# The beginning of an FFT filter and mixture-of-experts kernel laid out anew: larger loads of x, tables in order of use, one table made by transposes, weights later

## The chip, the cores and the metric

The kernel runs on one core of a Trainium2 chip. The metric is the device time of one execution in microseconds (us), the median of the runs shown; less is better.

## The reference

The input x has 8 sequences of 2496 rows and 256 channels. Each channel is filtered along its sequence in the frequency domain, and each filtered row then goes through one of 8 experts (a two-layer network), chosen by a gate.

```python
X = np.fft.rfft(x, axis=1)                    # x: 8 x 2496 x 256
y = np.fft.irfft(X * (filt_r + 1j * filt_i), n=2496, axis=1)
x = y.reshape(8 * 2496, 256)
logits = x @ w_gate                           # 256 x 8
probs = softmax(logits); e = argmax(logits)   # gate weight = probs[e]
out = probs[e] * (np.maximum(x @ w1[e], 0.0) @ w2[e])   # w1: 256 x 1024, w2: 1024 x 256
```

## The kernel before, in words

**The filter.** 2496 = 39 x 64, so the transform is done in two stages with matmuls. The work is cut into 16 units (u = 0 to 15): a sequence and one half of its channels. A unit has 5 iterations; t = 5u + it counts them from 0 to 79, and t is also the scale on which the whole program is ordered. For a unit, `loadx` (L231) brings x into tiles of 117 partitions (three groups of 39 rows) by 128 channels, and `forward1` (L249, matmul L257) multiplies by the small table `a1`; ScalarE, and for one of the six banks VectorE, copies the result out of PSUM into T (L265). A bank is up to 4 groups of x. For an iteration `spec1` transposes T (`pt`, L296) and ScalarE copies it to z (L302); `spec2` multiplies z by the second-stage table `bm` (`px`, L311); `filt_` multiplies by the filter `ff` on VectorE (`tr` and two halves of `ti`, L330 to L332); `join` adds the two on GpSimd (`p`, L339); `spec3` multiplies by the table `cm` (`pi`, L350), and ScalarE copies the result into the output tile U (L355). There are four tiles U0 to U3, a unit u using U(u mod 4).

**The tables.** `bm` and `cm` are 128 x 20 x 128 in f32, 0.26 MB for the four rows of an iteration, 1.31 MB each in all. `ff` holds the two parts of the filter: a DMA fills partitions 0 to 31 and 32 to 63 of it (L278 to L282), and `twice` (L287, instructions L289) copies them to partitions 64 to 127 on ScalarE, the second part with its sign turned, four rows (one iteration) at a time. Both units of a sequence and all sequences use the same tables. By construction cm for a row is the transpose of bm for it, except row 0.

**x in the beginning.** x goes through a pool of 4 buffers (`xp`) of one bank each, three DMAs of 78 KB to a bank. The load of a fifth bank waits until the first has been multiplied.

**The weights.** The experts' 16 weight matrices (0 to 15, w1 and w2 of each expert) are prepared while the filter runs: load (L373), VectorE maximum (L383), a turn through TensorE (`pw`, L406, and `pv`, L416) to get the maximum over partitions, split into a high half on ScalarE (L449) and a low half on VectorE (L454), and a write to a table `wscr` in HBM (L466, L468). In the order matrix q stands at t = 2.0 + 4.3 q.

**Behind it.** Once both units of a sequence are done its rows are routed, transformed to the time domain (`pg` L617, `py` L631) and scattered to `xs` in HBM by GpSimd (L158). From about t = 80 on the expert blocks are computed (`ph` L1014, `po` L1040) with weights loaded from `wscr` (L961).

**What sets the order.** All engines' queues are written out ahead of time, in the order of one list of steps, each with a key on the scale of t; `at(key, step)` puts a step there, and each engine goes through its part strictly in turn. So a step that must wait holds up all later steps of that engine, DMA issues on SyncE (SP) among them. What precedes t = 0 (the first loads, seven matmuls on a zero tile named `warm` at L750, the first unit's `forward1`) stands ahead of the list.

Of the kernel before, what the change touches and what calls it, by code (L numbers as in the profile page):

```python
# [9 lines left out]
F32 = mybir.dt.float32  # L10
# [5 lines left out]
ALU = mybir.AluOpType  # L16
# [11 lines left out]
GP = 3 * N1  # L28
# [85 lines left out]
def tile_fft_moe(ctx, tc, x, filt_r, filt_i, w_gate, w1, w2, cst, out):  # L114
    nc = tc.nc
# [24 lines left out]
    ident = cp.tile([128, 128], F32, name="ident")  # L140
# [44 lines left out]
    with ExitStack() as fctx:  # L185
# [42 lines left out]
        Uf = [u.rearrange("p n r -> p (n r)") for u in U]  # L228

        xt = {}  # L230

        def loadx(u, c):
            b, h = divmod(u, 2)
            xv = x[b].rearrange("(n1 n2) d -> n1 n2 d", n2=N2)[
                :, :, h * 128 : (h + 1) * 128
            ]
            t = xp.tile([GP, 4, 128], F32, name=f"x{u}_{c}", tag="x")
            g0, g1 = BANKS[c]
            for l in range(3):
                n = min(g1, NG if l == 0 else NG - 1) - g0  # L240
                s0 = 3 * g0 + l
                nc.sync.dma_start(
                    t[l * N1 : (l + 1) * N1, :n, :],
                    xv[:, s0 : s0 + 3 * (n - 1) + 1 : 3, :],
                )
# [24 lines left out]
        stk = {}  # L270
        ff = kp.tile([128, 2, 20, D], F32, name="ff")

        def loadf(k0, k1):

            n0 = max(k0, 1)
            for i, f in enumerate((filt_r, filt_i)):
                v = f[0:1248, :].rearrange("(j k) d -> j k d", k=N1)
                nc.sync.dma_start(ff[0:32, i, k0:k1], v[:, k0:k1, :])  # L278
                if k0 == 0:
                    nc.sync.dma_start(ff[32:33, i, 0], f[1248:1249, :])  # L280
                    nc.sync.dma_start(ff[33:64, i, 0], f[0:31, :])
                nc.sync.dma_start(  # L282
                    ff[32:64, i, n0:k1], v[:, 39 - n0 : 39 - k1 : -1, :]
                )

        def twice(k0, k1):

            for i, c in enumerate((1.0, -1.0)):
                nc.scalar.mul(ff[64:128, i, k0:k1], ff[0:64, i, k0:k1], c)  # L289
# [441 lines left out]
        def loadk(t, n, i0, i1, eng=nc.sync):  # L731
            eng.dma_start(t[:, 4 * i0 : 4 * i1], cst[n][:, 4 * i0 : 4 * i1])
# [24 lines left out]

        def consts():
# [21 lines left out]
        NU_ALL = 2 * B  # L780
# [3 lines left out]
        def at(key, f, *a):  # L784
            work.append((key, f, a))
# [14 lines left out]
                )  # L800


        K = {"s2": 1.394, "sr": 1.65, "si": 1.85, "s3": 3.6, "f": 0.063, "fd": 0.75, "w": 2.0, "wp": 4.3}
        RT = (0.0, 0.4, 0.45, 0.9, 1.3, 1.7, 2.2, 2.5, 2.9, 3.3)
        slow = lambda t: min(1.0, max(0.6, 1.0 - 0.06 * (t - 72)))
        for t in range(NT):
            u, it = divmod(t, 5)
            rho = slow(t)
            at(t, spec1, t)
            at(t + K["s2"] * rho, spec2, t)  # L810
            at(t + K["sr"] * rho, filt_, t)
            at(t + K["si"] * rho, join, t)
            at(t + K["s3"] * rho, spec3, t)
            if u + 1 < NU_ALL and it == 0:
                for j in range(6):
                    at(t + K["f"] + K["fd"] * j, forward1, u + 1, j)
            if u + 1 < NU_ALL and it == 0:
                for j in range(6):

                    n = 6 * (u + 1) + j - 4  # L820
                    v, i = divmod(n, 6)
                    at(5 * (v - 1) + K["f"] + K["fd"] * i + 0.02 if v else 0.01 + 0.02 * i, loadx, u + 1, j)
        for i in range(1, 5):
            if i > 1:
                at(0.1, loadk, bm, "bm", i, i + 1)
            if i % 2:
                at(0.09, loadf, 4 * i, 4 * i + 8)
            at(i - 0.1, twice, 4 * i, 4 * i + 4)
            at(0.1, loadk, cm, "cm", i, i + 1)

        PLACE = (80.0, 89.2, 109.2)
        done = []
        for b in range(B):
            rho = slow(10 * b + 9)
            s0 = 10 * b + 9 + K["s3"] * rho + 0.05
            c = 1.0 if b < B - 1 else 0.6
# [261 lines left out]
        for b in range(NB):  # L1098
            z, d, s = tau[b]
# [68 lines left out]
```

## Time and profile before

| what | value |
|---|---|
| median of 3 runs | 1451.44 us (1448.37, 1451.44, 1458.49) |
| the profiled execution | 1451.84 us, of which the span is 1450.1 us |
| TensorE (PE) matmul busy | 1334.0 us, 92% of the span |
| VectorE (DVE) busy | 823.5 us, 57% |
| ScalarE (ACT) busy | 855.7 us, 59% |
| GpSimd (POOL) busy | 456.3 us, 31% |
| PE busy in the first 60 us | 39.26 us |

The profile counts its times from the start of the span; the 1.74 us between the span and the execution's time lie around it. In rows of the timeline the first number is the start, the second the length, and what stands in brackets is the engine's idle time just ahead and what ended it. A matmul of f32 shows as two records, so that the four matmuls of a bank or of an iteration read as x8; a transpose shows as one, x4. PEclk is the granted TensorE clock, 1.00 at full speed. SPq is SyncE's queue, on which most DMAs are issued.

### The profile page before, as it was taken

The page shows a single profiled execution, that of the slowest core. Times are in us where ns is not written, and L with a number is a line of the kernel's source. Part 1 is how long each engine was busy: PE and PEld are TensorE (multiplying, and loading weights), DVE is VectorE, ACT ScalarE, POOL GpSimd, SP SyncE. Part 2 cuts the span into 40 slices and gives each one's busy share as a digit, 9 for nine tenths or more (in the row PEclk, how much of TensorE's full clock was granted, in tenths as well). Part 3 has the DMA queues.
Part 4 walks back from the last instruction along what each step waited for, and adds up shares of the span by engine and source line. Part 5 has one row for each costly group of instructions (what it writes and reads, how often), then busy time and mean ns, then how long its engine had stood idle before and what let it go on. Part 6 is the DMA issues. An engine that isn't in the chain of part 4 may idle for free.

```text
span 1450.1 us, 39859 instructions
## 1 busy us (share of the span) xinstructions
PE 1334.0 (92%) x14831; PEld 1189.0 (82%) x14831; DVE 823.5 (57%) x2381; ACT 855.7 (59%) x1449; POOL 456.3 (31%) x445
## 2 busy tenths in 40 slices
PE   5789999999989797789999998999999999999997
PEld 4777777777767576579999987998998998998997
DVE  0677878777676465245555554554554554554552
ACT  4557667666656554345666655565665655666564
POOL 1126484554737623521111111111111111111111
PEclk7799999999999899989999999999999999999999
DMA  7665565454533522367364289436436337234531
GB/s 193 177 189 175 165 180 171 156 172 152 170 120 113 178 67 68 94 185 201 75 160 111 74 231 329 108 77 161 102 78 188 72 79 187 74 78 125 137 78 42
DMA packets 199215, 199.07 MB, mean 137 GB/s; under 512 B 104259, under 2 KB 177652, under 8 KB 190700
## 3 DMA queue, kind: packets, MB, share of 16 engines
q1 hardware_dynamic: 179500, 153.80, 38.6%
q0 software_dynamic: 19520, 42.71, 10.5%
q8 instruction: 118, 1.93, 0.6%
q14 instruction: 77, 0.63, 0.2%
HBM read 347.54 MB, written 61.56 MB: 282 GB/s over the span
## 4 chain that ended last, share of the span: by engine, by line
PE 59%; DMA 6%; issue 4%; DVE 4%; ACT 2%; SPq 1%; POOL 1%; POOLq 0%; DVEq 0%; ACTq 0%
PE ph L1014 26%; PE po L1040 25%; DMA wb<-wscr 2%; PE py L631 2%; DMA wa<-wscr 2%; PE pi L350 1%; PE px L311 1%; PE pg L617 1%; PE f L257 1%; DMA xs<-yt,dest 1%; DVE hl L1028 1%; PE pt L296 1%; SPq L919 1%; DMA xt<-xs 0%; PE plw L481 0%
## 5 line engine op out<-in xcount | busy, mean ns | idle before, releaser
L1014 PE MATMUL ph<-xt,wa 128*128 128x128 f16 x7728 | 464.0, 219 | 28.1 <-DMA wa<-wscr 14.6
L1014 PEld LDWEIGHTS <-wa 128*128 128x128 f16 x7728 | 446.5, 98 | 41.3 <-issue 19.6
L1040 PE MATMUL po<-wb,hh 128*128 128x256 f16 x2576 | 435.3, 274 | 6.9 <-issue 2.6
L1028 DVE TENSOR_TENSOR hl<-hs,hh 128x512 f16<-128x512 f32 x322 | 223.7, 695 | 380.5 <-ACT hh L1022 316.6
L158 POOL DMA_INDIRECT out_dram<-ot,t x161 | 158.2, 983 | 696.7 <-DVE xs L994 621.6
L1040 PE MATMUL po<-wb,hl 128*128 128x256 f16 x1288 | 352.7, 274 | 3.1 <-issue 3.1
L1040 PEld LDWEIGHTS <-hh 128*128 128x128 f16 x2576 | 246.1, 98 | 40.4 <-issue 11.2
L1020 ACT ACTIVATE hs<-ph 128x512 f32<-128x512 f32 x322 | 191.8, 596 | 128.3 <-PE ph L1014 87.4
L158 POOL DMA_INDIRECT xs<-yt,dest x176 | 179.4, 1019 | 127.4 <-issue 56.7
L993 ACT ACTIVATE xs<-xb,s 128x256 f16<-128x256 f32 x161 | 81.8, 508 | 228.6 <-DVE s L983 224.0
L1022 ACT CAST hh<-hs 128x512 f16<-128x512 f32 x322 | 198.9, 618 | 10.1
L339 POOL TENSOR_TENSOR p<-tr,ti 128x512 f32<-128x512 f32 x80 | 107.1, 1338 | 160.2 <-DVE ti L332 120.2
L1040 PEld LDWEIGHTS <-hl 128*128 128x128 f16 x1288 | 126.5, 98 | 20.0 <-issue 4.9
L257 PE MATMUL f<-a,x 117*128 117x117 f32 x704 | 107.4, 297 | 26.0 <-DMA x<-in_x_dram 19.6
L257 PEld LDWEIGHTS f<-a,x 117*128 117x128 f32 x704 | 96.3, 209 | 32.7 <-issue 18.0
L355 ACT COPY U<-pi 128x512 f32<-128x512 f32 (+1 forms) x80 | 87.0, 1088 | 59.2 <-PE pi L350 44.8
L994 DVE SCALAR_TENSOR_TENSOR xs<-xb,s,xs 128x256 f16<-128x256 f32 x161 | 78.6, 488 | 53.5 <-ACT xs L993 53.1
L631 PE MATMUL py<-gh,dm 117*117 117x512 f32 x176 | 95.1, 622 | 8.9 <-ACT yt L633 6.5
L265 ACT COPY T<-f 128x468 f32<-128x468 f32 (+1 forms) x80 | 70.5, 881 | 51.6 <-PE f L257 50.7
L311 PEld LDWEIGHTS px<-z,bm 128*128 128x128 f32 x640 | 83.9, 201 | 15.4 <-issue 12.3
L350 PE MATMUL pi<-cm,p 128*128 128x128 f32 (+1 forms) x640 | 90.2, 286 | 4.8 <-POOL p L339 3.5
L311 PE MATMUL px<-z,bm 128*128 128x128 f32 x640 | 91.0, 288 | 0.2
(163 smaller groups left out, 1279.7 us busy)
## 6 DMA issues: line engine op xcount, KB each, us to landing
wb<-wscr SPq DMA_DIRECT2D x134, 1040.0 KB
wa<-wscr SPq DMA_DIRECT2D x134, 1024.0 KB
xb<-xs SPq DMA_DIRECT2D x161, 130.0 KB
x<-in_x_dram SPq DMA_DIRECT2D x240, 78.0 KB
wf<-in_moe_w_dram SPq DMA_DIRECT2D x32, 512.0 KB
wscr<-wh SPq DMA_DIRECT2D x8, 1040.0 KB
wscr<-wh SPq DMA_DIRECT2D x8, 1024.0 KB
xs<-yt,dest POOLq DMA_INDIRECT x176
```

Of the source, the lines that this page charges most:

```text
L158: nc.gpsimd.indirect_dma_start(out=dst, out_offset=bass.IndirectOffsetOnAxis(ap=idx, axis=0), in_=src, in_offset=None, bounds_check=bound, ...
L257: nc.tensor.matmul(ps[:, n : n + m], lhsT=xt.pop((u, g))[:m], rhs=a1[:m, :m], start=True, stop=True,)
L311: nc.tensor.matmul(ps[:, kk], lhsT=bm[:, 4 * it + kk], rhs=z[:, kk], start=True, stop=True,)
L339: nc.gpsimd.tensor_tensor(p, tr, ti, op=ALU.add)
L350: nc.tensor.matmul(ps[:, o : o + n], lhsT=p[:, kk], rhs=cm[:, k, :n], start=True, stop=True)
L355: nc.scalar.copy(U[u % NU].rearrange("p n r -> p r n")[:, r0 : r0 + o // 64, :], ps[:, :o].rearrange("p (r n) -> p r n", n=N2),)
L631: nc.tensor.matmul(ps[:GP], lhsT=dm, rhs=gh[:GP], start=True, stop=True)
L1014: nc.tensor.matmul(ps[:, f], lhsT=w[:, p : p + 128], rhs=xt[:, r, c], start=(n == 0), stop=(n == 5))
L1020: nc.scalar.activation(s, ps, AF.Relu, scale=1.0 / B23)
L1022: nc.scalar.copy(hh, s)
L1028: nc.vector.tensor_tensor(hl, s, hh, op=ALU.subtract)
L1040: nc.tensor.matmul(ps, lhsT=h2[q][:, f % 4], rhs=wv[:, r, f], start=(f == 0 and n == 0), stop=(f == 7 and n == 2),)
```

## The change

- x of units 0 and 1 is loaded in three pieces each (8, 11 and 3 groups) instead of six banks; the first two pieces go straight into tiles U2 and U3, which are not written before unit 2. Units from 2 on load as before.
- The first rows of bm and ff are issued on ScalarE's queue; the others on SyncE's, in the order of use. One small load of ff is dropped and a zero fill of it added.
- cm is not loaded but for row 0 (64 KB, on GpSimd's queue). A new step `flip` transposes bm's rows on TensorE into PSUM, and ScalarE copies them to cm: 3 transposes for iteration 0, 4 for each of the others.
- `twice` goes from ScalarE to GpSimd.
- 12 matmuls on the zero tile instead of 7.
- The small constants go from t = 0.9 to 4.6, and the weights from t = 2.0 + 4.3 q to 6.0 + 4.1 q.

```diff
+        HEAD = ((0, 8), (8, 19), (19, 22))
-        def loadx(u, c):
+        def loadx(u, c, eng=(nc.sync,) * 3):
...
-            t = xp.tile([GP, 4, 128], F32, name=f"x{u}_{c}", tag="x")
-            g0, g1 = BANKS[c]
+            g0, g1 = (HEAD if u < 2 else BANKS)[c]
+            if u < 2 and c < 2:
+                t = Uf[2 + u][:GP, 128 * g0 : 128 * g1]
+                t = t.rearrange("p (g d) -> p g d", d=128)
+            else:
+                t = xp.tile([GP, 4, 128], F32, name=f"x{u}_{c}", tag="x")
...
-        def loadf(k0, k1):
+        def loadf(i0, i1, eng=nc.sync):
+            k0, k1 = 4 * i0, 4 * i1
...
-        def twice(k0, k1):
-            for i, c in enumerate((1.0, -1.0)):
-                nc.scalar.mul(ff[64:128, i, k0:k1], ff[0:64, i, k0:k1], c)
+        def twice(it):
+            k = slice(4 * it, 4 * it + 4)
+            nc.gpsimd.tensor_copy(ff[64:128, 0, k], ff[0:64, 0, k])
+            nc.gpsimd.tensor_scalar(
+                ff[64:128, 1, k], ff[0:64, 1, k], -1.0, None, op0=ALU.mult
+            )
+
+        def flip(it):
+            ps = pA.tile([128, 4, 128], F32, name=f"pc{it}", tag="pF")
+            j0 = 0 if it else 1
+            for j in range(j0, 4):
+                nc.tensor.transpose(ps[:, j], bm[:, 4 * it + j], ident)
+            nc.scalar.copy(cm[:, 4 * it + j0 : 4 * it + 4], ps[:, j0:])
...
         nc.gpsimd.dma_start(a1, cst["a1"])
+        for c in range(3):
+            loadx(0, c)
+        loadk(bm, "bm", 0, 1, nc.scalar)
         nc.gpsimd.dma_start(ident, cst["ident"])
-        loadk(bm, "bm", 0, 1, nc.gpsimd)
-        loadx(0, 0)
-        loadx(0, 1)
-        loadf(0, 4)
-        loadx(0, 2)
-        loadx(0, 3)
-        loadk(bm, "bm", 1, 2)
-        loadk(cm, "cm", 0, 1)
+        nc.gpsimd.dma_start(cm[:, 0], cst["cm"][:, 0])
+        nc.vector.memset(ff[32:64, :, 0], 0.0)
+        loadf(0, 1, nc.scalar)
...
-        for i in range(7):
+        for i in range(12):
             nc.tensor.matmul(ps, lhsT=warm[:, :128], rhs=warm, start=True, stop=True)
         for j in range(6):
             forward1(0, j)
-            if j < 2:
-                loadx(0, j + 4)
-        twice(0, 4)
+        loadx(1, 0)
+        loadk(bm, "bm", 1, 2)
+        loadf(1, 2)
+        loadx(1, 1)
+        loadx(1, 2)
+        twice(0)
+        flip(0)
...
         for i in range(1, 5):
-            if i > 1:
-                at(0.1, loadk, bm, "bm", i, i + 1)
-            if i % 2:
-                at(0.09, loadf, 4 * i, 4 * i + 8)
-            at(i - 0.1, twice, 4 * i, 4 * i + 4)
-            at(0.1, loadk, cm, "cm", i, i + 1)
+            at(i - 0.5, twice, i)
+            at(i + 0.5, flip, i)
+        at(0.05, loadk, bm, "bm", 2, 4)
+        at(0.06, loadf, 2, 4)
+        at(1.9, loadk, bm, "bm", 4, 5)
+        at(1.91, loadf, 4, 5)
...
-            at(max(z - 3.2, 0.2 + 0.3 * q), w_load, e, i)
+            at(z - 3.2, w_load, e, i)
...
-        at(0.9, consts)
+        at(4.6, consts)
```

In the table K of the order, `"w": 2.0` becomes 6.0 and `"wp": 4.3` becomes 4.1.

What this does to the engines' queues shows at three places. The first is SyncE, from the loads of unit 1's x to the first weights (`x_3_254` is bank 3 of unit 1, `wf` a weight matrix). Before, the rows of ff and cm and bm that a line of dots replaces repeat the ones shown:

```order
L242 DMA x_2_235<-in_x_dram 39x4x128 x3
L278 DMA ff<-in_filt_r_dram 32x2048
L282 DMA ff<-in_filt_r_dram 32x8x256
L278 DMA ff<-in_filt_i_dram 32x2048
L282 DMA ff<-in_filt_i_dram 32x8x256
...
L732 DMA cm<-c_cm_dram 128x512
L732 DMA bm<-c_bm_dram 128x512
...
L242 DMA x_3_254<-in_x_dram 39x4x128 x3
L373 DMA wf_0_258<-in_moe_w_dram 128x1024 x2
```

And now, from the second piece of unit 1's x (`U_125` is tile U3, `x_0_271` bank 0 of unit 2):

```order
L248 DMA U_125<-in_x_dram 39x11x128 x3
L248 DMA x_2_208<-in_x_dram 39x3x128
L248 DMA x_2_208<-in_x_dram 39x2x128 x2
L747 DMA bm<-c_bm_dram 128x1024
L285 DMA ff<-in_filt_r_dram 32x2048
L288 DMA ff<-in_filt_r_dram 32x8x256
L285 DMA ff<-in_filt_i_dram 32x2048
L288 DMA ff<-in_filt_i_dram 32x8x256
L248 DMA x_0_271<-in_x_dram 39x4x128 x3
```

All of unit 1's x now stands ahead of the tables of iterations 2 and 3, where before bank 3 stood behind all tables. The second place is GpSimd, at its first sums p. Before (`p_313` is p of t = 0, `p_348` that of t = 1):

```order
L766 MEMSET go 128x176
L767 MEMSET go 128x8
L339 ISA
L339 TENSOR_TENSOR p_313<-tr_308,ti_309 128x512
L339 TENSOR_TENSOR p_348<-tr_343,ti_344 128x512
```

And now (`p_280` is p of t = 0, `p_326` that of t = 1; each pair of L293 and L294 is `twice` of one iteration, from iteration 0 on):

```order
L293 COPY ff<-ff 64x1024
L294 ISA
L294 TENSOR_SCALAR ff<-ff 64x1024
L293 COPY ff<-ff 64x1024
L294 TENSOR_SCALAR ff<-ff 64x1024
L293 COPY ff<-ff 64x1024
L294 TENSOR_SCALAR ff<-ff 64x1024
L354 TENSOR_TENSOR p_280<-tr_275,ti_276 128x512
L293 COPY ff<-ff 64x1024
L294 TENSOR_SCALAR ff<-ff 64x1024
L354 TENSOR_TENSOR p_326<-tr_317,ti_318 128x512
```

`twice` of iterations 0, 1 and 2 now stands ahead of the first p, that of iteration 3 ahead of the second. The third place is TensorE between bank 2 of unit 1 and the first `pi`. Before:

```order
L257 MATMUL f_1_2_298<-a_112,x_2_235 128x117 x4
L296 MATMUL pt_317<-ident,T_110 128x128 x4
L257 MATMUL f_1_3_328<-a_112,x_3_254 128x117 x4
L311 MATMUL px_338<-z_291,bm 128x128 x4
L406 MATMUL pw_0_352<-ident,wm_0_261 1x128
L296 MATMUL pt_354<-ident,T_110 128x128 x4
L257 MATMUL f_1_4_362<-a_112,x_4_231 128x117 x4
L311 MATMUL px_376<-z_322,bm 128x128 x4
L416 MATMUL pv_0_381<-wm_0_261,one 128x1
L350 MATMUL pi_383<-cm,p_313 128x64
```

And now:

```order
L263 MATMUL f_1_2_265<-a_112,U_125 128x117 x4
L311 MATMUL pt_287<-ident,T_110 128x128 x4
L263 MATMUL f_1_3_294<-a_112,U_125 128x117 x4
L326 MATMUL px_304<-z_250,bm 128x128 x4
L303 MATMUL pc_309<-ident,bm 128x128 x4
L311 MATMUL pt_328<-ident,T_110 128x128 x4
L263 MATMUL f_1_4_335<-a_112,U_125 128x117 x3
L263 MATMUL f_1_4_335<-a_112,x_2_208 128x117
L326 MATMUL px_345<-z_292,bm 128x128 x4
L303 MATMUL pc_350<-ident,bm 128x128 x4
L365 MATMUL pi_358<-cm,p_280 128x64
```

The turns of the first weight matrix (`pw`, `pv`) are gone from here, and the transposes for cm (`pc`) are new.

More of the change, by code (lines that the diff above doesn't have):

```diff
@@ L241, in loadx @@
                 s0 = 3 * g0 + l
-                nc.sync.dma_start(
+                eng[l].dma_start(
                     t[l * N1 : (l + 1) * N1, :n, :],
@@ L277, in loadf @@
                 v = f[0:1248, :].rearrange("(j k) d -> j k d", k=N1)
-                nc.sync.dma_start(ff[0:32, i, k0:k1], v[:, k0:k1, :])
+                eng.dma_start(ff[0:32, i, k0:k1], v[:, k0:k1, :])
                 if k0 == 0:
[L280 to L284, printed above, removed]
-        def twice(k0, k1):
-            for i, c in enumerate((1.0, -1.0)):
-                nc.scalar.mul(ff[64:128, i, k0:k1], ff[0:64, i, k0:k1], c)
+                    eng.dma_start(ff[32:33, i, 0], f[1248:1249, :])
+                eng.dma_start(ff[32:64, i, n0:k1], v[:, 39 - n0 : 39 - k1 : -1, :])
+        def twice(it):
[10 more added lines that the diff above has]
+            nc.scalar.copy(cm[:, 4 * it + j0 : 4 * it + 4], ps[:, j0:])
         def spec1(t):
@@ L800, in tails @@
                 )
-        K = {"s2": 1.394, "sr": 1.65, "si": 1.85, "s3": 3.6, "f": 0.063, "fd": 0.75, "w": 2.0, "wp": 4.3}
+        K = {"s2": 1.394, "sr": 1.65, "si": 1.85, "s3": 3.6, "f": 0.063, "fd": 0.75, "w": 6.0, "wp": 4.1}
         RT = (0.0, 0.4, 0.45, 0.9, 1.3, 1.7, 2.2, 2.5, 2.9, 3.3)
@@ L816, in tile_fft_moe @@
                     at(t + K["f"] + K["fd"] * j, forward1, u + 1, j)
-            if u + 1 < NU_ALL and it == 0:
+            if 0 < u and u + 1 < NU_ALL and it == 0:
                 for j in range(6):
@@ L821, in tile_fft_moe @@
                     v, i = divmod(n, 6)
-                    at(5 * (v - 1) + K["f"] + K["fd"] * i + 0.02 if v else 0.01 + 0.02 * i, loadx, u + 1, j)
+                    at(5 * (v - 1) + K["f"] + K["fd"] * i + 0.02, loadx, u + 1, j)
         for i in range(1, 5):
-            if i > 1:
-                at(0.1, loadk, bm, "bm", i, i + 1)
-            if i % 2:
-                at(0.09, loadf, 4 * i, 4 * i + 8)
-            at(i - 0.1, twice, 4 * i, 4 * i + 4)
-            at(0.1, loadk, cm, "cm", i, i + 1)
+            at(i - 0.5, twice, i)
[4 more added lines that the diff above has]
+        at(1.91, loadf, 4, 5)
         PLACE = (80.0, 89.2, 109.2)
```

## The prediction

> **What bounds the kernel now.** I read the page's shares first, then busy time by stretch, then TensorE's timeline of the first 70 us with the queues beside it. Busy time by stretch (busy us and instructions in brackets for PE, weight load, VectorE, ScalarE, GpSimd; then the granted clock, the DMA engines' share, GB/s):
>
> ```profile
> 2.00:7.00 5.00, 3.92 (x14) 2.01 (x12) 0.00 (x0) 0.97 (x2) 1.89 (x8) 1.00 0.83 226
> 0.00:28.00 28.00, 20.61 (x95) 17.15 (x95) 2.58 (x4) 11.05 (x12) 2.77 (x12) 0.70 0.70 176
> 28.00:33.00 5.00, 0.00 (x0) 0.00 (x0) 0.70 (x2) 4.39 (x5) 1.26 (x1) 0.96 1.04 187
> 34.00:38.00 4.00, 0.00 (x0) 0.00 (x0) 0.00 (x0) 0.00 (x0) 0.00 (x0) 0.50 1.05 380
> 38.00:40.00 2.00, 0.00 (x0) 0.00 (x0) 0.00 (x0) 0.00 (x0) 0.00 (x0) 0.50 1.13 237
> 100.00:500.00 400.00, 364.24 (x2603) 294.09 (x2602) 296.59 (x604) 259.95 (x388) 235.93 (x218) 0.97 0.51 160
> ```
>
> From 100 us on PE is busy 91% (364.24 of 400) and VectorE 74%; PE sets the pace. The beginning is different: nothing runs on PE from 28 to 40 us while the DMA engines are full, and before 28 us they are only 70% busy. So the beginning waits for data, in a poor order. TensorE's timeline names the wait:
>
> ```profile
> 12.75 6.74 PE L257 MATMUL f<-a,x 117*128 117x117 f32 x28 [3.50 <-DMA x<-in_x_dram]
> ...
> 27.23 0.60 PE L296 MATMUL pt<-ident,T 128*128 128x128 f32 x4
> 41.95 2.03 PE L257 MATMUL f<-a,x 117*128 117x117 f32 x8 [14.12 <-DMA x<-in_x_dram]
> 43.77 1.93 PE L311 MATMUL px<-z,bm 128*128 128x128 f32 x8
> 46.52 0.66 PE L296 MATMUL pt<-ident,T 128*128 128x128 f32 x4
> 50.19 0.72 PE L257 MATMUL f<-a,x 117*128 117x117 f32 x4
> 56.86 2.06 PE L257 MATMUL f<-a,x 117*128 117x117 f32 x8 [2.91 <-ACT z L302]
> 58.72 1.93 PE L311 MATMUL px<-z,bm 128*128 128x128 f32 x8
> 60.44 1.91 PE L350 MATMUL pi<-cm,p 128*128 128x128 f32 x8
> 62.15 1.61 PE L257 MATMUL f<-a,x 117*128 117x117 f32 x8
> 63.59 0.60 PE L296 MATMUL pt<-ident,T 128*128 128x128 f32 x4
> 64.03 1.06 PE L311 MATMUL px<-z,bm 128*128 128x128 f32 x8
> 64.93 1.05 PE L257 MATMUL f<-a,x 117*128 117x117 f32 x8
> 65.81 1.06 PE L350 MATMUL pi<-cm,p 128*128 128x128 f32 x8
> ```
>
> The 14.12 us are bank 3 of unit 1's x. Each idle stretch is paid twice, since the clock falls: starts of steps lie 1.7 us apart at 60 us and 0.9 us at 64 us (a transpose step 0.45 us). The clock rises 4 to 4.6 us after work resumes at 41.95, and 6.3 us after 56.86. The 2.91 us at 56.86 come from ScalarE, which did `twice` just then; SyncE's queue shows why bank 3 was late:
>
> ```profile
> 54.20 2.00 ACT L289 ACTIVATE ff<-ff 64x1024 f32<-64x1024 f32 x2
> 24.78 0.57 SPq L732 DMA_DIRECT2D cm<-c_cm_dram  x1
> 33.69 0.33 SPq L732 DMA_DIRECT2D cm<-c_cm_dram  x1
> 35.11 1.37 SPq L242 DMA_DIRECT2D x<-in_x_dram  x3
> SPq L732 <- DMA ff<-in_filt_r_dram: 3.6, 3, 2.0
> ```
>
> Seven loads of cm and bm (1.83 MB) stood ahead of bank 3, and they in turn waited for ff. Bank 3 went out at 35.11, and its last bytes arrived 7 us later.
>
> My mark for the sum is the start of `pi` of t = 3, at 65.81. From there the same steps follow in both kernels, with the weights one matrix later, so a gain at the mark goes through to the end unless something later takes it back.
>
> **The change part by part.** *Bytes.* Until the tables of iterations 2 and 3 are in, the changed kernel brings two units of x (2.56 MB), a1, ident and cm's row (0.19), bm of 0 to 3 (1.05) and ff of 0 to 3 (2.03): 5.82 MB; 1.31 MB of cm and the first weights (1.05 MB) are no longer in the way. Rates at full engines come from the rows above: 187 GB/s for ff (28 to 33 us), 380 for bm and cm (34 to 38), 237 for x (38 to 40). That is 10.8 + 0.8 + 2.8 + 10.9 = 25.3 us; counted from 2 us, where the first row of the stretches begins: 27.3. The loads of before left a trough when the first wave was in:
>
> ```profile
> 7.00:8.00 1.00, 0.07 (x1) 0.10 (x1) 0.00 (x0) 0.00 (x0) 0.00 (x0) 1.00 0.36 78
> 8.00:9.00 1.00, 1.00 (x8) 0.97 (x8) 0.00 (x0) 0.00 (x0) 0.00 (x0) 0.85 0.22 55
> SPq L281 <- DMA x<-in_x_dram: 1.3, 1, 1.3
> ```
>
> The queue waits there for older DMAs. I allow such a trough (1.4 us) and 1.3 us, the wait in that row, from the last bytes to the signal: 30.0 for the second half of ff of iterations 2 and 3; the first half 0.52 MB / 187 = 2.8 us earlier, about 27.5. Bounds: 27.3 if nothing is lost; if it goes at before's pace, 28 x 176 GB/s = 4.93 MB by 28 us and the other 0.89 MB at 187, it is 32.8, with 1.3 to the signal 34.1.
>
> The larger pieces of x, the second queue and the U tiles are inside this rate; alone I give them nothing. The 12 zero matmuls run while x is coming. Before, unit 0's first stage was through at 19.5 us (12.75 + 6.74); now x of unit 0, a1, ident, cm's row, bm and ff of iteration 0 (2.19 MB) are in by 2 + 2.19 MB / 226 = 11.7, and what PE does until the tables are in (unit 1's five banks, `pt`, `px`, the transposes for cm of iterations 0 to 3) has time until 30: all hidden. If that cover were gone, the 19 transposes would be 5 x 0.45 = 2.3 us of PE.
>
> *twice on GpSimd.* The trace has no such instruction there. Rows near it:
>
> ```profile
> L289 ACT ACTIVATE ff<-ff 64x1024 f32<-64x1024 f32 x10 | 10.1, 1049 | 2.1 <-DMA ff<-in_filt_i_dram 1.6 <-DMA ff<-in_filt_r_dram 0.4
> L339 POOL TENSOR_TENSOR p<-tr,ti 128x512 f32<-128x512 f32 x4 | 5.1, 1272 | 49.8 <-DVE ti L332 49.8
> 3.16 0.20 POOL L762 MEMSET wg<- 128x64 f32 x1
> 3.83 0.11 POOL L767 MEMSET go<- 128x8 f32 x1
> ```
>
> The same shape costs ScalarE 1.05 us; GpSimd needs 1.27 for 512 elements of two inputs, so 2.5 for 1024. One input instead of two speaks for the lower half; I take 1.6, bounds 1.05 and 2.5. On GpSimd the first p stands behind `twice` of iteration 2, so it now waits for ff of iterations 2 and 3, whose data it doesn't use. This is what is late next. First half in at 27.5, copied by 29.1; second half in at 30.0, done 31.6; p of t = 0 done at 32.9; then two instructions and a p each: 37.4, 41.9 (ff of iteration 4 is in by 35: 1.03 MB behind), the five memsets 0.8, p of t = 3 at 44.0.
>
> The Trainium skill's GPSIMD Engine Reference, Engine selection, says that one-input elementwise work on GpSimd runs at roughly line rate and two-input work about twice as slow as on VectorE. By it the copy would be near 1.05 and the chain 0.55 us per instruction shorter; no run here shows it yet.
>
> *PE from there.* PE has been idle for over 3 us, so it starts cold at 32.9: `pi` 1.7, bank 5 of unit 1 1.3, `pt` 0.9, `px` 1.7 and `pc` 0.9 lead to 39.4, about when the clock rises (32.9 + 6.3 = 39.2). Then `pi`, `pt`, unit 2's bank 0, `px` (0.9 + 0.45 + 0.9 + 0.9) to 42.6, `pi` (p is ready at 41.9), a bank, `pt`, `px`, a bank (0.9 + 0.9 + 0.45 + 0.9 + 0.9) to 46.6, and 0.4 for ScalarE's copies in between: `pi` of t = 3 at 47.0. The gain at the mark is 65.8 - 47.0 = 18.8 us. `twice` has also left ScalarE, which takes away the wait at 56.86; that is inside the 18.8.
>
> *Weights one matrix later.* Before, the first matrix was done by the mark; now it is not, and 16 rather than 15 lie in the rest. VectorE's share of one and its waits (groups from 100 to 500 us; waits; the last matrix):
>
> ```profile
> L454 DVE SCALAR_TENSOR_TENSOR wh<-wf,ws,wh 128x1024 f16<-128x1024 f32 x26 | 35.3, 1378 | 9.0 <-issue 4.5 <-DMA x<-in_x_dram 2.5 <-ACT wh L449 1.7
> L383 DVE TENSOR_REDUCE wm<-wf 128x1 f32<-128x1024 f32 x26 | 30.6, 1230 | 0.2
> PE pw L406 <- DVE wm L394: 7.6, 3, 3.8
> 425.87 0.59 PE L406 MATMUL pw<-ident,wm 128*1 128x128 f32 x2 [3.80 <-DVE wm L394]
> 426.38 2.08 PE L350 MATMUL pi<-cm,p 128*128 128x128 f32 x8
> 440.83 0.37 SPq L468 DMA_DIRECT2D wscr<-wh  x1
> 471.51 0.34 SPq L961 DMA_DIRECT2D wa<-wscr  x1
> ```
>
> The four long instructions are 2 x 1.38 + 2 x 1.23 = 5.2 us of VectorE. Hidden in its idle 26% they cost nothing, all on the path 5.2, and a wait of PE as at 425.87 adds 3.8; I take 2.0, nearer to hidden because PE, not VectorE, sets the pace there; bounds 0 and 9. The last write to `wscr` goes one t later (6 us at most); the first load from it is 30 us behind, so no wait arises. The constants moved to t = 4.6 are first used after t = 8, with no cost.
>
> **The sum** is made against the profiled execution, 1451.84 us (its span 1450.1 and 1.7 around it), 0.4 above the median: 1451.8 - 18.8 + 2.0 = 1435.0 us.
>
> **The rivals.**
>
> *GpSimd becomes the bound of the beginning.* With 2.5 us per instruction p of t = 2 comes at 46.4 (30.0 + 2.5 + 1.3 + 2 x 6.3), and `pi` of t = 3 follows 4.1 us later, at 50.5: gain 15.3, time 1438.5; with the late bound of the data as well, 1442. For it: GpSimd's only measured elementwise row. Against: it has two inputs.
>
> *Everything a little better.* GpSimd at 1.05, the clock up after 4 us as it was after 41.95, data at 28.5, the weights hidden: p of t = 0 at 30.9, `pi` of t = 3 at about 44, time 1451.8 - 21.8 = 1430; a shift of a few stalls between 100 and 500 us, where PE idles 36 us in all, reaches 1424. The Trainium skill's TensorE: Matmul & The Clock Gate, Part 1, says that the clock is released after about 3.4 us of sustained work; by it the cold part would be 1 to 1.5 us cheaper still. Both rises in this trace took longer.
>
> *The weights' turns land badly (slower).* With 4.1 in place of 4.3 each of the 16 turns meets another neighbour. In this trace 3 after 60 us make PE wait, up to 3.8 us, and the clock falls after the longest (the `pi` at 426.38 takes 2.08), some 3 us more. At 7 us a hit the third further hit takes it past the time of before (1435 + 21 = 1456), and five make 1470. For it: VectorE is the busier of the helpers. Against: its order around the turns is as before, and only one of the 16 was that dear.
>
> *The end hangs on something else.* If the expert blocks were held by what does not move, the time stays at 1451. Against: their first matmuls follow the filter's last units directly, and no clock-bound event lies there.
>
> **How the numbers follow.** Forecast as summed 0.52 (its own range 1430 to 1440, of which 0.40 lies below 1436.9), GpSimd as the bound 0.12, everything better 0.16, turns landing badly 0.14 (0.07 of it within 1%, 0.06 slower, 0.01 still faster), nothing moves 0.06. About 1% is what a measurement of this kernel can tell from no change: 1436.9 or less counts as faster. Faster 0.40 + 0.16 + 0.01 = 0.57; within 1% 0.12 + 0.12 + 0.07 + 0.06 = 0.37; slower 0.06. The range takes in 1424 of the better case and reaches up to 1447, past GpSimd as the bound with late data and into the bad turns.
>
> **What would show it.** Right: no idle stretch over 2 us on PE for unit 1's x; one long idle stretch ahead of the first `pi`, ended by GpSimd's p at 31 to 35 us; GpSimd's p waiting for its own copies, those for DMA of ff; `pi` of t = 3 at 45 to 49 us; the expert blocks starting earlier by about the same. Wrong: the first `pi` later than 38 us (data or copies mispriced), or a gain at the mark that the stretch from 100 to 500 us gives back, with more PE waits at `pw`.

## The result, and the profile after

The changed kernel takes 1429.48 us (median of 4 runs, 1427.5 to 1430.49), the kernel before on the same chip 1450.51 (4 runs, 1448.37 to 1458.49): ratio 0.984, 95% interval 0.981 to 0.988. The profiled execution has a span of 1427.7 us against 1450.1. Faster, then, by 21 us, and 5.5 us below the forecast. But the time came from other places than the forecast said, as TensorE's timeline of the beginning shows first:

```profile
8.49 3.63 PE L263 MATMUL f<-a,U 117*128 117x117 f32 x16 [2.32 <-DMA U<-in_x_dram]
14.97 4.31 PE L263 MATMUL f<-a,U 117*128 117x117 f32 x22 [2.85 <-DMA U<-in_x_dram]
19.12 0.95 PE L263 MATMUL f<-a,x 117*128 117x117 f32 x6
...
26.89 1.12 PE L263 MATMUL f<-a,U 117*128 117x117 f32 x8 [2.06 <-DMA U<-in_x_dram]
...
39.89 2.07 PE L365 MATMUL pi<-cm,p 128*128 128x64 f32 x8 [5.63 <-POOL p L354]
...
50.26 1.16 PE L365 MATMUL pi<-cm,p 128*128 128x128 f32 x8 [0.66 <-POOL p L354]
...
54.50 1.07 PE L365 MATMUL pi<-cm,p 128*128 128x128 f32 x8
```

Of the 14.12 us for unit 1's x, 2.06 are left (at 26.89), and one wait of 5.63 us for GpSimd's first p stands in their place, as forecast. PE is busy 43.00 of the first 60 us; before, it is 35.26, not the 39.26 of the table ahead of the prediction. But the wait ends at 39.9, where 33 was forecast, and `pi` of t = 3, the mark, is at 54.50 (forecast 47.0, before 65.81). The large loads have not sped up unit 0 either: its first stage ends at 20.1 (19.12 + 0.95), before at 19.5. GpSimd's timeline gives the chain behind the wait:

```profile
33.02 1.03 POOL L293 COPY ff<-ff 64x1024 f32<-64x1024 f32 x1 [7.90 <-DMA ff<-in_filt_r_dram]
35.73 2.76 POOL L294 TENSOR_SCALAR ff<-ff 64x1024 f32<-64x1024 f32 x1 [1.68 <-DMA ff<-in_filt_i_dram]
38.58 1.26 POOL L354 TENSOR_TENSOR p<-tr,ti 128x512 f32<-128x512 f32 x1
39.90 1.03 POOL L293 COPY ff<-ff 64x1024 f32<-64x1024 f32 x1
40.91 2.76 POOL L294 TENSOR_SCALAR ff<-ff 64x1024 f32<-64x1024 f32 x1
43.76 1.26 POOL L354 TENSOR_TENSOR p<-tr,ti 128x512 f32<-128x512 f32 x1
```

The two halves of ff of iteration 2 are there at 33.0 and 35.7 (forecast 27.5 and 30.0), and the half with the sign turned takes 2.76 us, not 1.6, each time. The gain at the mark is therefore 65.8 - 54.5 = 11.3 us, not 18.8. The span shrank by 22.4; so some 11 us came later. Busy time by stretch shows where, first before, then after:

```profile
60.00:460.00 400.00, 367.44 (x2671) 301.47 (x2670) 307.38 (x608) 263.27 (x383) 222.84 (x202) 0.97 0.52 161
```

```profile
0.00:28.00 28.00, 18.82 (x105) 15.28 (x106) 3.78 (x6) 9.48 (x12) 9.74 (x11) 0.88 0.95 175
60.00:460.00 400.00, 371.28 (x2771) 302.40 (x2770) 327.29 (x648) 274.07 (x403) 230.95 (x212) 1.00 0.54 168
```

In 60 to 460 us PE's busy time is nearly the same, but it does 100 matmuls more in it: the granted clock is 1.00 instead of 0.97. By the clock's records the kernel before ran at half clock up to 63.3 us, which is still ahead of its mark, and then for 23.9 us in four falls, at 87, 224, 295 and 425 us; the changed kernel had none in this stretch. The fall at 224 shows what one is. TensorE's timeline of before, and its busy time in the stretch of the wait and the next:

```profile
224.27 0.40 PE L558 MATMUL pp<-oh,ltri 117*117 117x176 bf16 x1 [3.28 <-DVE oh L549]
```

```profile
220.30:223.70 3.40, 0.70 (x7) 0.50 (x5) 3.10 (x5) 3.29 (x5) 0.00 (x0) 1.00 0.24 65
223.70:227.10 3.40, 2.83 (x14) 2.83 (x15) 3.21 (x8) 0.59 (x1) 0.63 (x1) 0.51 0.01 2
```

PE waits 3.28 us for VectorE, and the next 6.8 us run at half clock. Two of the other three falls stand behind waits for VectorE at `pw` (87 and 425), one behind a wait at `pv` (295). PE's waits from 60 to 500 us, in total, times and longest (that of `pw` before stands in the prediction), before and after:

```profile
PE pp L558 <- DVE oh L549: 7.9, 6, 3.3
PE pv L416 <- DVE wm L411: 2.6, 2, 2.4
```

```profile
PE pp L573 <- DVE oh L564: 5.4, 5, 2.3
PE pw L421 <- DVE wm L409: 3.0, 4, 1.0
PE pv L431 <- DVE wm L426: 1.2, 2, 1.0
```

No wait for VectorE here is longer than 2.3 us any more. Fewer idle microseconds and a better clock could each make the 11 us; PE's busy time from the mark to the start of the last `tr`, which ends the filter, tells them apart (before, then after):

```profile
65.81:513.80 447.99, 404.43 (x2904) 329.37 (x2903) 330.65 (x672) 287.30 (x423) 257.15 (x235) 0.96 0.51 160
```

```profile
54.50:489.50 435.00, 394.80 (x2911) 321.43 (x2910) 341.32 (x684) 289.26 (x425) 256.15 (x235) 0.98 0.54 170
```

For nearly the same matmuls PE is busy 9.6 us less and idle 3.4 us less: most of these 13.0 us is the clock, a smaller part the waits themselves, and some 2 us are lost again behind the filter. Which edit did that is the question for the runs.

### The profile page after: what moved, and what is told of

The parts are those of the page before. It is cut to its first block, busy times and chain, and to the rows that moved or that the text cites. A ratio compares the mean times of both kernels' runs of the same rounds, so it can differ in the third digit from the quotient of the medians.

```text
span 1427.7 us, 39877 instructions
## 1 busy us (share of the span) xinstructions
PE 1323.9 (93%) x14855; PEld 1183.0 (83%) x14855; DVE 827.9 (58%) x2382; ACT 847.5 (59%) x1444; POOL 473.5 (33%) x455
## 4 chain that ended last, share of the span: by engine, by line
PE 56%; issue 5%; DMA 3%; ACT 2%; SPq 2%; DVE 2%; POOL 1%; POOLq 0%; ACTq 0%; DVEq 0%
PE ph L1031 27%; PE po L1057 25%; DMA wa<-wscr 3%; PE py L646 1%; SPq L936 1%; POOL xs L158 1%; PE pi L365 1%; PE pg L632 1%; DMA wb<-wscr 1%; SPq L1018 0%; DVE hl L1045 0%; PE px L326 0%; ACT U L370 0%; ACT hh L1039 0%; POOL out_dram L158 0%
## 5 line engine op out<-in xcount | busy, mean ns | idle before, releaser
L354 POOL TENSOR_TENSOR p<-tr,ti 128x512 f32<-128x512 f32 x80 | 103.9, 1299 | 102.1 <-DVE ti L347 82.6
L263 PE MATMUL f<-a,x 117*128 117x117 f32 (+1 forms) x628 | 87.6, 278 | 5.3 <-ACT U L370 2.7
L365 PEld LDWEIGHTS pi<-cm,p 128*128 128x128 f32 x640 | 79.8, 195 | 15.3 <-POOL p L354 11.4
L1073 ACT ACTIVATE ot<-po,g 128x256 f32<-128x256 f32 x161 | 73.5, 457 | 30.5 <-PE po L1057 13.4
```

Of the source, the lines that this page charges most:

```text
L263: nc.tensor.matmul(ps[:, n : n + m], lhsT=xt.pop((u, g))[:m], rhs=a1[:m, :m], start=True, stop=True,)
L354: nc.gpsimd.tensor_tensor(p, tr, ti, op=ALU.add)
L365: nc.tensor.matmul(ps[:, o : o + n], lhsT=p[:, kk], rhs=cm[:, k, :n], start=True, stop=True)
```

## The experiments

Three sets of four experiments, each set with the kernel before on its own chip: 1453.87 us (1449.43 to 1458.92) for E1 to E4, 1417.01 (1413.47 to 1421.39) for E5 to E8, 1452.47 (1447.99 to 1458.21) for E9 to E12. The second chip runs the kernel before some 36 us faster; ratios compare across sets, times do not.

**E1 and E2: the change without the weights' move, and the move alone.** E1 is the changed kernel with

```diff
-"w": 6.0, "wp": 4.1
+"w": 2.0, "wp": 4.3
...
-            at(z - 3.2, w_load, e, i)
+            at(max(z - 3.2, 0.2 + 0.3 * q), w_load, e, i)
...
-        at(4.6, consts)
+        at(0.9, consts)
```

and E2 the kernel before with the same three lines the other way round. The small constants move with the weights in both; no run moves them alone.

> The changed kernel with the weights and the small constants back at their old places in the order (2.0 + 4.3 q, constants at 0.9); the beginning stays new. Theory W: half of the gain comes from where the weights' turns fall, because with the old places VectorE makes TensorE wait long enough between 60 and 430 us for the clock to fall. Then cold stretches of about 20 us in all come back between 60 and 450 us and the time is 1441 us (1437 to 1446). Rival H: the new beginning alone makes the gain, the clock falls by chance: 1430 us, within 3.

> The kernel before with only the new places of the weights and the small constants (6.0 + 4.1 q, constants at 4.6). Theory W: the waits that let the clock fall between 60 and 450 us are gone, and one matrix less is in the beginning: 1438 us (1434 to 1442), with the idle stretch of about 14 us at bank 3 of unit 1 still there. Rival H: 1450 us, within 4.

E1: 1444.28 us (1440.55 to 1447.89), ratio 0.9935 (0.9912 to 0.9958). E2: 1434.65 (1433.13 to 1435.58), ratio 0.9873 (0.985 to 0.9896). Both lie where Theory W put them. The weights' move alone is worth 1.3%, the rest of the change alone 0.65%, both together 1.6%. What I had priced at a loss of 2 us is the larger part. In E1 four falls of the clock between 60 and 460 us are back, 13.7 us at half clock; in E2 there is none. TensorE's timeline of E1, where the first matrix's turn makes PE wait:

```profile
39.64 0.59 PE L421 MATMUL pw<-ident,wm 128*1 128x128 f32 x2 [8.40 <-DVE wm L409]
...
56.48 1.07 PE L365 MATMUL pi<-cm,p 128*128 128x128 f32 x8
```

and of E2:

```profile
39.76 2.03 PE L257 MATMUL f<-a,x 117*128 117x117 f32 x8 [15.03 <-DMA x<-in_x_dram]
...
51.31 1.15 PE L257 MATMUL f<-a,x 117*128 117x117 f32 x8 [0.42 <-ACT z L302]
...
57.46 1.07 PE L350 MATMUL pi<-cm,p 128*128 128x128 f32 x8
```

E2 still has the long idle time for bank 3, and yet its mark is 8.4 us earlier than before. Bank 3 arrives 2.2 us earlier (39.76 for 41.95), and the wait of 2.91 us at 56.86 with its half clock is gone (0.42 at 51.31). I had put that wait down to `twice` on ScalarE. ScalarE's timeline of before, ahead of the row at 54.20 that the prediction quotes, and that of E2 show that this was half of it:

```profile
51.78 1.15 ACT L449 ACTIVATE wh<-wf,ws 128x1024 f16<-128x1024 f32 x1 [0.40 <-DVE ws L427]
...
53.04 1.13 ACT L449 ACTIVATE wh<-wf,ws 128x1024 f16<-128x1024 f32 x1
```

```profile
48.64 2.00 ACT L289 ACTIVATE ff<-ff 64x1024 f32<-64x1024 f32 x2
```

Before, the first matrix's two high halves (2.3 us) stood in front of `twice`. Without them `twice` on ScalarE makes PE wait 0.42 us. E1 has it the other way round, the high halves on ScalarE without `twice`, and PE's only wait for z up to its mark is 0.16 us:

```profile
49.54 0.66 PE L311 MATMUL pt<-ident,T 128*128 128x128 f32 x4 [0.16 <-ACT z L317]
```

So the 2.91 us took both; with one of the two gone, so are they. Given the weights' move, the whole new beginning moves the mark only from 57.46 to 54.50, by 3.0 us.

**E3 to E5: what GpSimd costs in the beginning.** E3 puts `twice` later, E4 puts its sign-turning half on ScalarE (for iteration 0 right behind `twice`), E5 does both:

```diff
-            at(i - 0.5, twice, i)
+            at(i - 0.1, twice, i)      (E3 and E5)
...
-            nc.gpsimd.tensor_scalar(
-                ff[64:128, 1, k], ff[0:64, 1, k], -1.0, None, op0=ALU.mult
-            )
+        def turned(it):
+            k = slice(4 * it, 4 * it + 4)
+            nc.scalar.mul(ff[64:128, 1, k], ff[0:64, 1, k], -1.0)
...
+            at(i + 0.9, turned, i)     (E4 and E5)
```

> The changed kernel with each copy of the filter to partitions 64 to 127 one place later, behind the sum p of the iteration two before it, so that the first p no longer stands behind the copies of iteration 2. Theory P: the order on GpSimd is what holds TensorE for 5.6 us ahead of the first pi; the first p is then done at about 28 us instead of 39.8, TensorE does not wait there, and pi of t = 3 starts at 50 us instead of 54.5: 1425 us. Rival Q: GpSimd's total of work (five pairs of 3.8 us and the sums) sets the mark whatever the order: pi of t = 3 at 53 to 55 us, 1429 us.

> The changed kernel with the sign-turning half of the copies back on ScalarE, 0.9 of an iteration after its time, and the plain copies left on GpSimd where they were. Theory Q: GpSimd's 2.76 us multiplies are what is dear; the first p is done at about 35.5 us, p of t = 2 at 40 instead of 50.2, and pi of t = 3 starts at 46 us instead of 54.5: 1421 us. Theory P (the order alone): the first p still waits for the copy of iteration 2 until 34, so 1426 us, pi of t = 3 at 51 us.

> The changed kernel with the sign-turning half of twice on ScalarE (as in e4) and GpSimd's copies placed later, at i - 0.1 (as in e3). If what e4 left ahead of the first pi is still GpSimd's copies waiting for ff of iteration 2 (1.19 us of PE's wait there), moving them behind the first p takes that wait and no more: first pi at about 34, pi of t = 3 at 46 to 47, 1422 us (1420 to 1424). If instead the later copies hold up f of unit 2 as in e3 (3.7 us idle and a cold clock), pi of t = 3 goes back to 50 or later and the time to 1425 or more.

E3: 1428.05 (1426.18 to 1430.27), ratio 0.9821 (0.9797 to 0.9846). E4: 1423.35 (1422.9 to 1424.6), ratio 0.9795 (0.9772 to 0.9819). E5, on the second chip: 1389.66 (1386.5 to 1392.52), ratio 0.9813 (0.9778 to 0.9848). TensorE's timelines of E3 and of E4:

```profile
34.07 1.06 PE L365 MATMUL pi<-cm,p 128*128 128x64 f32 x8
...
45.30 1.12 PE L263 MATMUL f<-a,x 117*128 117x117 f32 x8 [3.71 <-issue]
...
52.82 1.07 PE L365 MATMUL pi<-cm,p 128*128 128x128 f32 x8
```

```profile
34.97 1.16 PE L367 MATMUL pi<-cm,p 128*128 128x64 f32 x8 [1.19 <-POOL p L356]
...
47.58 1.07 PE L367 MATMUL pi<-cm,p 128*128 128x128 f32 x8
```

In E3 the first `pi` comes 5.8 us earlier than in the changed kernel, the mark only 1.7, as its Rival Q said: the order of GpSimd's work gives the start, but its sum (5.1 us for an iteration, copy, multiply and p) sets the rest. The profile names no releaser for the 3.71 us ahead of the bank at 45.30. By the kernel's code that bank takes the PSUM buffer (the fourth before it in `pF`) from which VectorE's `ti` reads, and `ti` waits for GpSimd's multiply and is through at 45.20:

```profile
43.81 0.69 DVE L346 TENSOR_TENSOR ti<-px,ff 64x512 f32<-64x512 f32 x1 [2.05 <-POOL ff L294]
44.52 0.68 DVE L347 TENSOR_TENSOR ti<-px,ff 64x512 f32<-64x512 f32 x1
```

In E4, with the multiply off GpSimd, the mark is 6.9 us earlier than in the changed kernel, nearer to Theory Q's 46 than to Theory P's 51. E5 adds nothing to E4: the first `pi` is at 34.1, but PE then waits 2.3 us for ScalarE at the next bank, the clock falls, and the mark is at 49.3, nearer to its rival. GpSimd's multiply is thus the largest cost of the change that E3 to E8 find.

**E6 to E8: large loads, cm by transposes, the second queue, each undone.** E6 loads six pieces, the first five of each unit into U2 and U3; in E7 cm's first rows are loaded whole, too, and all transposes are gone.

```diff
-        HEAD = ((0, 8), (8, 19), (19, 22))                             (E6)
+        HEAD = ((0, 4), (4, 8), (8, 12), (12, 16), (16, 19), (19, 22))
...
-            at(i + 0.5, flip, i)                                       (E7)
+        at(0.07, loadk, cm, "cm", 1, 4)
...
+        at(1.92, loadk, cm, "cm", 4, 5)
...
-        loadk(bm, "bm", 0, 1, nc.scalar)                               (E8)
+        loadk(bm, "bm", 0, 1)
...
-        loadf(0, 1, nc.scalar)
+        loadf(0, 1)
```

> The changed kernel with x of units 0 and 1 loaded in six pieces of at most four groups, as before, though still into tiles U2 and U3 and in the same place of the order: only the size of the loads changes. Theory: the large pieces bring nothing, since the first f starts at 8.49 instead of 4.32 and unit 0's first stage ends 0.5 us later than before. Then the first f starts at 4 to 6, ff of iteration 2 lands within 1 us of where it does now, and the time is 1427 to 1431. Rival: many small loads fill the queue and leave troughs in it (as from 7 to 9 us before), ff of iterations 2 and 3 lands 2 us or more later, pi of t = 3 at 57 or later, time 1432 or more.

> The changed kernel with all of cm loaded by DMA (behind bm and ff of iterations 1 to 3, that of iteration 4 behind its ff) in place of the transposes. Theory: cm's 1.25 MB come while PE waits for GpSimd anyway, and the transposes lie in the same idle time: pi of t = 3 within 1 us of 54.5, time 1428 to 1431. Rival, the load is paid on the path: 1.25 MB at 380 GB/s is 3.3 us, pi of t = 3 at 57 to 58, time 1432 to 1434. Second rival, that the transposes cost: 16 at 0.45 us for four is 1.8 us, which would come back, 1427.

> The changed kernel with the first rows of bm and ff issued on SyncE's queue behind unit 0's x, in place of ScalarE's queue beside it. Theory: the DMA engines are full (share 0.95 up to 28 us) and one queue or two makes no difference: first f earlier by up to 3 us, since unit 0's x no longer shares with bm and ff, ff of iteration 2 within 1 us of where it lands now, time 1427 to 1431. Rival: the second queue is what keeps the engines full; then the share falls to 0.8 or less up to 28 us, ff lands 3 us or more later, time 1432 or more.

E6: 1396.97 (1394.37 to 1399.47), ratio 0.986 (0.9827 to 0.9893). E7: 1398.39 (1396.07 to 1403.43), 0.9883 (0.9847 to 0.9919). E8: 1396.36 (1394.82 to 1397.94), 0.9853 (0.9822 to 0.9884). All three intervals overlap those of the changed kernel (0.981 to 0.988, and 0.985 to 0.990 in E9), so in the whole time none of the three edits shows. The expected times are the first chip's and don't apply. The places are compared across chips, for no trace of the changed kernel was taken on this one: from the mark to the last `tr` E5 to E8 take 430.2 to 431.8 us, the change, E2 to E4 and E9 434.5 to 438.2, so about 1% more, or half a microsecond at the mark. TensorE's timelines of E6, E7 and E8:

```profile
13.82 1.04 PE L263 MATMUL f<-a,x 117*128 117x117 f32 x6
...
52.35 1.07 PE L365 MATMUL pi<-cm,p 128*128 128x128 f32 x8
```

```profile
39.45 2.07 PE L361 MATMUL pi<-cm,p 128*128 128x64 f32 x8 [8.16 <-POOL p L350]
...
53.92 1.07 PE L361 MATMUL pi<-cm,p 128*128 128x128 f32 x8
```

```profile
55.05 1.07 PE L365 MATMUL pi<-cm,p 128*128 128x128 f32 x8
```

E6: with small loads unit 0's first stage ends at 14.9 instead of 20.1, and the mark is 2.2 us earlier, more than the chip explains. The large loads cost a little, against my theory of no difference and the rival's opposite sign. E7: cm by DMA leaves the mark within 0.6 us; PE waits 8.16 us for GpSimd instead of 5.63, so the transposes only filled a wait. E8: one queue instead of two leaves the mark within 0.6 us. Both as their theories said.

**E9 to E12: start or period of the weights, and a better version.** E9 is the change unaltered. E10 and E11 change one number of the weights' order each, E12 is E4 with the small loads of E6 (its edit is theirs):

```diff
-"w": 6.0, "wp": 4.1
+"w": 6.0, "wp": 4.3      (E10)
+"w": 2.0, "wp": 4.1      (E11; loads and constants as in E1)
```

> The changed kernel unaltered, as the base of this set, since chips differ: ratio to before 0.984 (0.981 to 0.988), that is 18 to 27 us less than before on this chip; ff of iteration 2's multiply is done at 38 to 39, pi of t = 3 at 54 to 55.

> The changed kernel with the weights at 6.0 + 4.3 q: the start of the change, the period of before. Theory S, the late start is what helps: as the changed kernel of this set within 3 us, no cold stretch between 60 and 460 us. Theory P, it is where each turn falls among the steps (the period) that decides: 7 to 15 us above the changed kernel, cold stretches of 3.4 or 6.8 us between 60 and 460, each behind a wait of PE of over 1.8 us, as with 2.0 + 4.3 q.

> The changed kernel with the weights at 2.0 + 4.1 q (and the constants at 0.9, where they must be for it): the start of before, the period of the change. Theory S: as with 2.0 + 4.3 q, 10 to 18 us above the changed kernel of this set, with cold stretches between 60 and 460 us. Theory P: only the first matrix's turn in the beginning is paid again, pi of t = 3 at 56 to 57 instead of 54.5, and 1 to 5 us above the changed kernel, with no cold stretch between 80 and 460.

> The changed kernel with the sign-turning half of twice on ScalarE (as in e4) and x of units 0 and 1 in small pieces (as in e6). In e6 ff of iteration 2 was there at 30.4 for its copy, in e4 at 32.5; if the two add, first p is done at 32.8, first pi at 33 to 34, pi of t = 3 at 45 to 47, and the time 7 to 9 us below the changed kernel of this set, ratio to before 0.977 to 0.980. Rival: what then ends last is ScalarE, which has the copies of T, z and now the multiplies, in pieces that arrive sooner; pi of t = 3 stays at 47.6 or later and the time at 5 to 6 us below the changed kernel, as e4.

E9: 1432.37 (1430.77 to 1436.55), ratio 0.9874 (0.9847 to 0.99). E10: 1433.74 (1429.18 to 1444.05), 0.9888 (0.9853 to 0.9924). E11: 1441.7 (1435.31 to 1447.54), 0.9934 (0.9909 to 0.9959). E12: 1428.04 (1421.92 to 1430.97), 0.9824 (0.9795 to 0.9853).

By the medians the start counts, not the period: E10 takes the time of E9, and E11 has the ratio of E1 (0.9934 and 0.9935). But the intervals of E10 and E11 overlap, and in the profiled executions the two end the filter 0.9 us apart (table below). Neither theory is right on the clock: E10 has 10.2 us at half clock between 60 and 460 and E11 13.7, E9 3.4. In E11 the first matrix's turn costs the beginning again:

```profile
39.48 0.59 PE L421 MATMUL pw<-ident,wm 128*1 128x128 f32 x2 [8.57 <-DVE wm L409]
```

The waits for VectorE go with the period: between 60 and 460 us the longest at `pw`, `pv` or `pp` is 3.8, 3.3 and 4.5 us with 4.3 (before, E1, E10), and 1.6 us (E11) to 2.3 us in all runs with 4.1. The shorter ones do not save E11's clock, as two of its three falls lie behind waits for ScalarE, of 1.82 and 2.07 us. PE's waits at `pw` in E10, and TensorE's timeline of E11:

```profile
PE pw L421 <- DVE wm L409: 7.0, 4, 4.5
```

```profile
148.35 1.40 PE L496 MATMUL plw<-U,wg 128*32 128x351 f32 x8 [2.07 <-ACT U L370]
```

E9 shows why the clock is so hard to foresee. It is the same program as the changed kernel and has the same wait of 2.32 us at the same place, at 94.70 and at 95.00; timelines and busy time of E9, then of the change:

```profile
94.70 0.29 PE L573 MATMUL pp<-oh,ltri 117*117 117x176 bf16 x1 [2.32 <-DVE oh L564]
```

```profile
92.30:95.70 3.40, 1.08 (x11) 1.00 (x11) 3.19 (x9) 1.31 (x3) 0.00 (x0) 1.00 0.01 4
95.70:99.10 3.40, 3.40 (x11) 1.77 (x10) 3.22 (x9) 1.45 (x2) 1.27 (x1) 0.51 0.21 61
```

```profile
95.00 0.29 PE L573 MATMUL pp<-oh,ltri 117*117 117x176 bf16 x1 [2.32 <-DVE oh L564]
```

```profile
90.40:93.80 3.40, 2.28 (x21) 2.08 (x19) 3.26 (x8) 2.35 (x4) 1.38 (x2) 1.00 0.40 112
93.80:97.20 3.40, 2.20 (x17) 1.87 (x18) 3.21 (x9) 1.07 (x3) 0.00 (x1) 1.00 0.00 0
```

In each trace the falls of the clock lie a whole number of 3.413 us apart. On that grid the wait of E9 falls into one stretch, which leaves PE busy 1.08 of 3.4 us, and the next runs at half clock; in the change the grid cuts the same wait in two, PE is busy 2.28 and 2.20, and the clock stays. I cut all 14 traces into stretches on their own grid, from 60 to 470 us: of the stretches begun at full clock, all 24 with PE busy less than 45% were followed by half clock, 5 of 23 with 45 to 55%, none above that.

E12 shows the same from the other side: its mark is at 47.00, 7.2 us earlier than E9's, but in its profiled execution, the slowest of its six, two stretches with PE busy 40 and 44% put 10.2 us at half clock. The median is 4.3 below E9, not the 7 to 9 expected. E3, E4, E5 and E12 have the best ratios, 0.980 to 0.982; their intervals do not tell them apart.

Two terms account for most of the gain at the end of the filter (the start of the last `tr`, 513.8 us before): the gain at the mark, and half of the half-clock time that went away between the mark and 465 us (23.9 us before). In us, for the runs on chips of one pace:

| kernel | mark | half clock left | mark + half of what went | last `tr` earlier by |
|---|---|---|---|---|
| the change | 11.3 | 0 | 11.3 + 12.0 = 23.3 | 24.3 |
| E1 | 9.3 | 13.7 | 9.3 + 5.1 = 14.4 | 10.7 |
| E2 | 8.4 | 0 | 8.4 + 12.0 = 20.4 | 21.8 |
| E3 | 13.0 | 3.4 | 13.0 + 10.3 = 23.3 | 24.1 |
| E4 | 18.2 | 3.4 | 18.2 + 10.3 = 28.5 | 28.1 |
| E9 | 11.6 | 3.4 | 11.6 + 10.3 = 21.9 | 23.1 |
| E10 | 9.9 | 10.2 | 9.9 + 6.9 = 16.8 | 16.9 |
| E11 | 9.7 | 13.7 | 9.7 + 5.1 = 14.8 | 16.0 |
| E12 | 18.8 | 10.2 | 18.8 + 6.9 = 25.7 | 23.9 |

Seven of nine agree within 1.5 us, E12 within 1.8; E1 is off by 3.7. Why the times go with the start while the waits for VectorE go with the period, the runs do not settle; each order meets other waits. Behind the filter a part is lost again: the span shrinks by 22.4 us for the change, 7.3 for E1 and 18.7 for E2, and from the last `tr` on the clock's records have 37.1, 35.1 and 34.9 us at half clock, before 28.4.

## Why the prediction was right and wrong

The sum was 1451.8 - 18.8 + 2.0; the measured terms are -11.3 and about -11. The forecast was near because two wrong sizes cancelled, which is luck, not because its account was right. One of its own signs of being wrong came: the first `pi` stands at 39.9, later than 38, and the mark at 54.5 is outside 45 to 49. Nor are the two terms separate, as the sum has them: of the 11.3 us at the mark the weights' move alone gives 8.4 (E2), the rest of the change alone 9.3 (E1).

- **What bounds the beginning, and the new wait:** right. One wait for GpSimd's p stands ahead of the first `pi`, its copies wait for ff, and the transposes for cm and the second queue are hidden (E7, E8).
- **The bytes and their rate** ("30.0 for the second half"): failed, and it is 5.7 of the 7.5 us by which the mark was missed. I had taken full engines to mean 187 to 380 GB/s, each kind of load at its rate in an undisturbed stretch. The share did rise to 0.95, but the first 28 us moved 175 GB/s, as before with a share of 0.70. Even the late bound, 34.1, was passed. x of unit 2's first bank (0.24 MB), which I had not counted, goes out right behind the last piece of ff, by SyncE's queue, and so can move beside it. The queue, and busy time up to 1.3 us ahead of the second half's multiply:

```profile
26.77 0.31 SPq L288 DMA_DIRECT2D ff<-in_filt_i_dram  x1
27.30 2.42 SPq L248 DMA_DIRECT2D x<-in_x_dram  x3
```

```profile
0.00:34.40 34.40, 24.34 (x151) 20.40 (x151) 6.83 (x10) 12.94 (x18) 10.77 (x12) 0.90 0.96 176
```

By an estimate from these rows, 34.4 us at 176 GB/s are 6.05 MB, and the prediction's 5.82 with the 0.24 are 6.06; its 1.3 us to the signal make 35.7, when the multiply begins. The first tables of iteration 4, issued from 30.85 us on, are left out of it.

- **`twice` on GpSimd** (1.6 each): the copy is 1.03, the multiply 2.76, above my upper bound of 2.5. It cost 1.2 us at the first p and 0.7 for each further iteration; E4 takes it away and gains 6.9 at the mark. The Trainium skill's GPSIMD Engine Reference, Engine selection, which puts one-input work at roughly line rate, agrees with the copy and not with the multiply.
- **The wait at 56.86, put down to `twice`:** half right. The wait is gone without `twice` on ScalarE (E1, which has the rest of the new beginning too, 0.16 us), but also without the first matrix's high halves in front of it (E2, 0.42 us).
- **Weights one matrix later, +2.0, bounds 0 and 9:** the sign failed. I counted VectorE's work that is moved into the rest, and not the waits of PE that it leaves when the turns fall elsewhere. A gain had been left out of the bounds for no reason; the row at 425.87, a wait of 3.80 us with slow matmuls behind it, showed that the turns of before already cost something, and what a fall costs stood under the rival "turns land badly", with only its loss counted. The half clock between the mark and 465 us, 23.9 us before, is 0 after, worth about 12 at half its length and 9.6 by PE's busy time.
- **Large pieces of x at nothing:** right within the time's interval, though they cost the mark up to 2 us (E6).
- **The gain at the mark goes through to the end:** right up to the filter's end (table), with the clock adding up to 12 us on the way; behind it the change keeps 22.4 of 24.3 us. E12 lost most of what it had gained over E9 there.

The rival "GpSimd becomes the bound", at 1438.5, was right about the place: E3 shows that GpSimd's sum decides. "Everything a little better", at 1430, had the time, but of its conditions only the hidden weights and the copy's 1.05 us (1.03) held: the multiply took 2.76, the data came at 35.7 instead of 28.5, and the clock rose 6.1 us after 39.89, not 4. "The weights' turns land badly" named the right place with the wrong sign: the period of 4.1 that it feared goes with the shorter waits for VectorE.

## What to carry to other kernels

A short wait of the busiest engine can cost more behind it than in itself: before pricing a move of helper work, list the waits over about 1.7 us (half of the 3.4 us stretch) that it could end or make, with the clock in the next stretch of the profile. Where two edits can explain one gain, do each alone; here the edit that seemed a side effect was alone worth twice the rest of the change. A full share of the DMA engines is no rate: take the bytes that a like mixture of loads moved, not the best rate of each.

## What the runs showed of the hardware that was not expected

- The clock is halved for 3.4 us or a multiple of it after a stretch of 3.413 us, on a fixed grid, in which PE was busy less than about half (24 of 24 stretches below 45%, 5 of 23 from 45 to 55%, none above); a wait of 2.32 us is enough or not by where it stands on the grid (E9 and the change). The Trainium skill's TensorE: Matmul & The Clock Gate, Part 1, describes such a free-running window of 3413 ns, and these traces agree with the length; it gives an idle window as what slows the clock, and here a window half idle did.
- GpSimd's multiply by a constant took 2.76 us where its copy of the same 64x1024 f32 took 1.03, and ScalarE's multiply 1.05.
- A higher share of the DMA engines moved no more bytes: in the first 28 us the change has a share of 0.95 and 175 GB/s, before 0.70 and 176, and E6, the change with small loads of x, on the second chip, 0.76 and 185, by its busy time by stretch:

```profile
0.00:28.00 28.00, 18.86 (x125) 14.56 (x126) 5.52 (x9) 11.66 (x15) 9.75 (x11) 1.00 0.76 185
```
